# The first four tiles of each attention layer turned on TensorE, a written order for the first steps, and a flag check moved into the last filter's loop

## The chip, the cores and the metric

One Trainium2 chip, one core. TensorE (PE) multiplies matrices and can transpose 128x128 blocks; VectorE (DVE), ScalarE (ACT) and GpSimd (POOL) do the rest; SyncE (SP) issues nearly all DMAs. The metric is the device time of one execution in microseconds (us). The kernel before took 3790.33 us, the median of three runs (3786.84 to 3791.4).

## The reference

Two times attention and then a spectral filter, each on a layernormed input and added to it. Weights are the same in both layers.

```
x: (1, 2048, 1024)    32 heads of 32    float32
x = x + attn(layernorm(x));  x = x + filt(layernorm(x))     # twice
attn(x): q, k, v = x @ wqkv;  softmax(q k^T / sqrt(32)) v;  @ wo
filt(x): irfft2(rfft2(x) * (w_r + i w_i))
layernorm(x) = (x - mean) / sqrt(var + 1e-5)
```

## The kernel before

x lies in SBUF as 16 tiles of 128 rows by 1024 columns (`ap.x`, in the trace R). Float32 products are made of float16 halves: a number is split into a high part (`hi`, on ACT) and what is left (`lo`, on DVE), and a product is hi·hi + hi·lo + lo·hi (`split`, L167 and L168).

**The attention's prologue.** Each tile goes through `ln`: BN_STATS on its two halves (L111, L112), an aggregation, the root of the variance by a power on POOL (L120) and one Newton step on DVE (L121 to L124), a bias `lb`; then ACT writes the normed tile `xn` (L334), the split makes `hl` (hi and lo in float16), and two DMA transposes (L339) put them, turned, into `big`, the arrays `xh` and `xl` of four chunks of 512 rows. Out of these PE makes sums of 48 products for two tiles of v (`v_tiles`, L401; v0 to v7), and of 24 products for one chunk of k or q (`qk_chunk`, L357; k0 to k3, q0 to q3). Their order on PE is v0 v1 k0 q0 v2 k1 q1 v3 k2 q2 v4 k3 q3, the sums of the norms (L374), v5 v6, the first scores S (L586), v7. The norms go by POOL to a bias (L387) that the first exponential (L590) needs. In layer 0 the x tiles and the weights come by DMA meanwhile, in layer 1 x is in place and is written to memory beside the transposes (L341).

The sums use two PSUM banks by turns, `x` (v0, k0, v2, q1, ...) and `o` (v1, q0, k1, v3, ...). A sum starts only when the one before it in its bank is read out: v2 waits until k0's high part (ACT) and its low part (DVE, L168, written R<-x) have been taken. K's, Q's and V's first arrays lie in x's own tiles 0 to 7, so k0 may be taken out only when ACT has read tiles 6 and 7 for their xn.

The order on each engine is fixed when the kernel is built. In the prologue a scheduler chooses it by its own estimates of when things are ready; each engine then goes through its row in order and waits where something isn't ready. From the attention's main loop on (S, exp, PV at L596, sums at L609) the order is written out.

**The spectral filter** ends each layer. Its second part is a loop over 32 units (36 steps with the run-in and run-out), each with a weight load on SP (`loadw`), products on PE and three engines that follow; then come 16 steps of transposes and products (L982, L994), whose last adds to x are the rows L1005 to L1013. In layer 0 these adds are followed by layer 1's statistics.

**The flags.** Beside the work the kernel gathers whether a value left the range for which the split is good. `combine_flags` joins them after the last filter: two small PE instructions (L1161, L1166), DVE rows between and behind them, a conversion to an integer `fi` (L1170), and on every engine a load of it into a register (L1171) and a branch (L1223) round a general version that is not run here.

```
both banks:   bank(): odd calls psX ("x"), even calls psO ("o")
SP, layer 0:  x0 x1 wv(4 loads) wk(2) x2.. x5 ...   one x load per tile in ln
```

## Time and profile before

| what | value |
|---|---|
| median of three runs | 3790.33 us (3786.84 to 3791.4) |
| the profiled execution | 3789.62 us, of which the span is 3787.7 |
| PE busy | 3694.6 us (98%) |
| DVE busy | 3179.3 us (84%) |
| ACT busy | 2893.2 us (76%) |
| layer 0: first matmul, first S | 18.62, 111.37 us |
| layer 1: last adds of filter 0, first matmul, first S | 1893.81, 1908.19, 1994.18 us |
| last matmul of the last filter, end of span | 3774.83, 3787.7 us |

A row of the timeline reads: start, duration (both us), engine, line, operation, out<-in with the shapes, how many instructions the row groups, and in square brackets how long the engine had been idle ahead of it and what ended that. A row of the windows gives a stretch's bounds and length, the busy time (and instructions) of PE, of PE's weight loads, of DVE, ACT and POOL, the clock granted to PE as a part of full speed, the busy share of the DMA engines and GB/s.

### The profile page before, as it was taken

The page shows a single profiled execution, that of the slowest core. Times are in us where ns is not written, and L with a number is a line of the kernel's source. Part 1 is how long each engine was busy: PE and PEld are TensorE (multiplying, and loading weights), DVE is VectorE, ACT ScalarE, POOL GpSimd, SP SyncE. Part 2 cuts the span into 40 slices and gives each one's busy share as a digit, 9 for nine tenths or more (in the row PEclk, how much of TensorE's full clock was granted, in tenths as well). Part 3 has the DMA queues.
Part 4 walks back from the last instruction along what each step waited for, and adds up shares of the span by engine and source line. Part 5 has one row for each costly group of instructions (what it writes and reads, how often), then busy time and mean ns, then how long its engine had stood idle before and what let it go on. Part 6 is the DMA issues. An engine that isn't in the chain of part 4 may idle for free.

```text
span 3787.7 us, 79598 instructions
## 1 busy us (share of the span) xinstructions
PE 3694.6 (98%) x32951; PEld 1640.7 (43%) x32951; DVE 3179.3 (84%) x3824; ACT 2893.2 (76%) x3567; POOL 308.2 (8%) x386
## 2 busy tenths in 40 slices
PE   7999999999999999999989999999999999999998
PEld 4433433343344233378953334333433432333798
DVE  6799899989999988955658998999899999789554
ACT  5688888888888866658747888888888888666696
POOL 1000000000000000014410000000000000000143
PEclk9999999999999999999999999999999999999999
DMA  8000000000000211233270010001000002111433
GB/s 209 15 18 18 13 12 18 24 10 18 12 24 11 94 48 65 79 124 119 69 184 15 29 34 24 29 26 35 14 29 29 33 14 93 54 70 67 156 98 106
DMA packets 166868, 202.58 MB, mean 53 GB/s; under 512 B 75104, under 2 KB 120928, under 8 KB 165472
## 3 DMA queue, kind: packets, MB, share of 16 engines
q1 hardware_dynamic: 166208, 197.34, 16.3%
q8 instruction: 260, 4.26, 0.5%
q14 instruction: 112, 0.92, 0.1%
q10 hardware_dynamic: 288, 0.07, 0.0%
HBM read 132.35 MB, written 48.23 MB: 48 GB/s over the span
## 4 chain that ended last, share of the span: by engine, by line
PE 85%; DVE 6%; issue 4%; ACT 2%; DMA 1%; POOL 1%; SPq 0%; DVEq 0%; POOLq 0%; ACTq 0%
PE o L596 23%; PE s L586 19%; PE x L357 15%; PE x L401 7%; PE x L459 6%; PE ps L879 3%; PE s L459 2%; DVE R L609 2%; PE ps L823 2%; PE s L616 2%; PE ps L948 1%; PE ps L911 1%; PE ps L814 1%; PE ps L994 1%; PE ps L982 1%
## 5 line engine op out<-in xcount | busy, mean ns | idle before, releaser
L590 ACT ACTIVATE p<-s,bias 128x1024 f32<-128x1024 f32 x2048 | 2168.7, 1112 | 569.1 <-PE s L586 553.2
L609 DVE TENSOR_TENSOR R<-R,p 128x1024 f32<-128x1024 f32 x1792 | 2087.2, 1218 | 130.9 <-ACT p L590 127.6
L596 PE MATMUL o<-p,R 128*32 128x512 f32 x8192 | 985.0, 598 | 0.0
L357 PE MATMUL x<-big,wqk 128*128 128x512 f16 x2880 | 676.4, 380 | 1.7 <-ACT R L405 0.9
L586 PEld LDWEIGHTS <-R 32*128 32x128 f16 x12288 | 230.7, 92 | 752.9 <-issue 636.8
L357 PEld LDWEIGHTS <-wqk 128*128 128x128 f16 x3072 | 275.7, 98 | 419.6 <-issue 131.3
L596 PEld LDWEIGHTS o<-p,R 128*32 128x32 f32 x8192 | 213.7, 109 | 523.3 <-issue 523.3
L586 PE MATMUL s<-R 32*128 32x512 f16 x6144 | 430.2, 378 | 5.2 <-ACT p L590 3.3
L586 PE MATMUL s<-Q,R 32*128 32x512 f16 x6144 | 427.3, 377 | 4.6 <-DVE R L500 2.6
L401 PE MATMUL x<-wv,big 128*128 128x256 f16 x2784 | 331.8, 276 | 33.3 <-DMA big<-hl 33.3
L401 PEld LDWEIGHTS <-big 128*128 128x128 f16 x3072 | 292.8, 99 | 135.1 <-issue 58.6
L459 PE MATMUL x<-big 128*128 128x512 f16 x1050 | 241.6, 380 | 0.0
L382 POOL PARTITION_ALL_REDUCE mall<-mqk x16 | 45.2, 2826 | 2281.5 <-DVE mqk L376 2269.9
L459 PEld LDWEIGHTS <-big 128*128 128x128 f16 x1344 | 124.3, 98 | 176.4 <-issue 38.6
L607 DVE SCALAR_TENSOR_TENSOR R<-p 128x1024 f32<-128x1024 f32 x128 | 150.7, 1218 | 34.6 <-ACT p L590 34.6
L927 DVE TENSOR_TENSOR H<-G,H 128x512 f16<-128x512 f32 (+1 forms) x68 | 47.1, 692 | 116.6 <-ACT H L926 116.4
L872 ACT COPY U<-ps 64x256 f32<-64x256 f32 (+1 forms) x272 | 97.0, 357 | 9.4 <-PE ps L879 4.1
L879 PE MATMUL ps<-cbi,H 128*128 128x256 f16 (+1 forms) x792 | 98.8, 273 | 4.0 <-ACT H L926 2.7
L872 ACT COPY B<-ps 64x256 f32<-64x256 f32 (+1 forms) x272 | 97.0, 357 | 6.7 <-PE ps L879 3.2
L617 DVE STREAM_TRANSPOSE zt<-s 128x512 f32<-128x512 f32 x64 | 45.7, 714 | 62.8 <-PE s L616 62.7
L879 PE MATMUL ps<-cb,big 128*128 128x256 f16 x780 | 96.2, 273 | 0.0
L828 DVE TENSOR_TENSOR big<-ps,big 128x512 f16<-128x512 f32 x64 | 44.5, 695 | 57.8 <-ACT big L827 57.8
(431 smaller groups left out, 2952.0 us busy)
## 6 DMA issues: line engine op xcount, KB each, us to landing
wst<-in_wp SPq DMA_DIRECT2D x96, 256.0 KB, 3.1
R<-y SPq DMA_DIRECT2D x32, 512.0 KB, 5.2
w<-in_w SPq DMA_DIRECT2D x60, 256.0 KB, 2.6
od<-ohl SPq DMA_DIRECT2D x56, 256.0 KB, 2.4
big<-od SPq DMA_DIRECT2D x16, 896.0 KB, 6.4
y<-R SPq DMA_DIRECT2D x20, 512.0 KB, 2.6
R<-in_x SPq DMA_DIRECT2D x16, 512.0 KB, 5.8
wst<-in_wo SPq DMA_DIRECT2D x32, 256.0 KB, 2.9
```

Source lines behind the costliest of these rows:

```text
L357: nc.tensor.matmul(ps, a, b, start=d == 0 and i == 0, stop=d == 7 and i == 2)
L401: nc.tensor.matmul(ps[:, j], l, r, start=d == 0 and i == 0, stop=d == 7 and i == 2)
L459: nc.tensor.matmul(p, a, b, start=start and d == ds[0] and i == 0, stop=stop and d == ds[-1] and i == 2)
L586: nc.tensor.matmul(s[h // 2][:, h % 2], K[g][r, a, kt * 128:kt * 128 + 128], Q[g][r, b, c * 512:c * 512 + 512], start=i == 0, stop=i == 2)
L590: nc.scalar.activation(p, s[hf], AF.Exp, bias=bias[g], scale=SCALE / (SQ * SQ))
L596: nc.tensor.matmul(O[g, c][32 * h:32 * h + 32], V[g][:, kt, 32 * h:32 * h + 32], P[g, c, kt, h // 2][:, h % 2], start=kt == 0, stop=kt == ...
L607: nc.vector.scalar_tensor_tensor(acc[hf], P[g, c, 0, hf], 1e-34, p, op0=ALU.add, op1=ALU.add)
L609: last_add = nc.vector.tensor_add(acc[hf], acc[hf], p)
L616: nc.tensor.matmul(z[32 * h:32 * h + 32], cst["ones"], acc[h // 2][:, h % 2], start=True, stop=True)
L823: nc.tensor.matmul(pa[:, j], tt[:, j], mm[:, g], start=True, stop=True)
L872: nc.scalar.copy(ov[64 * r:64 * r + 64, a0:a0 + m, x], tl[64 * x:64 * x + 64, :m, r])
L879: nc.tensor.matmul(out, l, r, start=k == 0, stop=k == len(mm_) - 1)
```

## The change

Four things are changed.

1. Tiles 0 to 3 of both layers are turned on PE: eight float32 transposes of `xn` into PSUM (`turn_x`), out of which ACT takes the high and DVE the low part straight into `xh` and `xl` (`split_x`). `hl` and the DMA transposes stay for tiles 4 to 15.
2. These first steps have an order written out on PE, DVE and ACT. On DVE the Newton step of tile t+1 stands behind the low part of tile t (for tile 1 ahead of tile 0's), on PE the turn of tile t+1 stands between the matmuls of v0 or v1. In layer 1 tile 0's statistics and root stand among the last adds of filter 0. The rest of the prologue has a written order on PE alone; its other work is let go when the fourth tile's split has been issued (`issue_after`).
3. The sums run xh·w_hi (8 products), xh·w_lo (8), xl·w_hi (8) and no longer alternate. norm(k) stands ahead of 24 matmuls of v5, norm(q) behind them. SP's x loads stand early and in a row (x0, the four of wv, x1 to x3, wk, x4, wq, x5 to x15); in layer 1 the writes of x stand ahead of the transposes instead of beside them. The five looks for flags on the weights follow the prologue's last low part.
4. `combine_flags` is called in step 20 of the last filter's loop; at the end only the register load stays.

```diff
-    v, r, q = (sm.tile([128, n], F32, name=f"{c}{n}") for c in "vrn")
+def ln_pow(nc, sm, cst, mv, eng, n=1):
...
+def ln_newton(nc, sm, v, r, eng, n=1):
...
+def tile_root(nc, ap, cst, flags, layer, t):
+
+    mv = tile_stats(nc, ap, flags, layer, t)
+    v, r = ln_pow(nc, ap.sm, cst, mv, nc.vector)
+    yield
+    ln_newton(nc, ap.sm, v, r, nc.vector)
+    flags["rb"] = r, ln_bias(nc, ap.sm, mv, r)
+    yield
...
+    def save_x(ts):
+        for t in ts if layer else ():
+            nc.sync.dma_start(xin[t * 128:(t + 1) * 128, :], ap.x[:, t])
...
+    def turn_x(xn):
+        p = psS.tile([128, 2, 512], F32, name="s").rearrange("p h (d n) -> p (h d) n", n=128)
+        for d in range(8):
+            nc.tensor.transpose(p[:, d], xn[:, 128 * d:128 * d + 128], cst["ident"])
+        return p
+
+    def split_x(t, p, n):
+        c, o = t // 4, (t % 4) * 128
+        for d in range(0, 8, n):
+            r = split(nc, xh[c][:, d:d + n, o:o + 128], xl[c][:, d:d + n, o:o + 128], p[:, d:d + n], SX)
+        return r
...
-            if layer:
-                nc.sync.dma_start(xin[t * 128:(t + 1) * 128, :], ap.x[:, t])
...
+        for i, (a, b) in enumerate([(w[:, n, d], x[c][:, d]) for x, n in ((xh, 0), (xh, 1), (xl, 0)) for d in range(8)]):
+            nc.tensor.matmul(ps, a, b, start=i == 0, stop=i == 23)
...
+    with tc.manual_schedule(engines={mybir.EngineType.PE, mybir.EngineType.DVE, mybir.EngineType.Activation}):
...
+        xn = norm_x(0, *flags.pop("rb"))
+        for t in range(4):
+            p = turn_x(xn)
+            if t < 3:
+                m = tile_root(nc, ap, cst, flags, layer, t + 1)
+                next(m)
+                run(pre[0])
+                if t == 0:
+                    next(m)
+            ends = split_x(t, p, 4 if t == 0 else 8)
+            if t % 2:
+                if t < 3:
+                    next(m)
+                    xn = norm_x(t + 1, *flags.pop("rb"))
+                run(vk.pop(0))
+            else:
+                if t:
+                    next(m)
+                xn = norm_x(t + 1, *flags.pop("rb"))
+                steps(vk[0], 8)
+    with tc.manual_schedule(engines={mybir.EngineType.PE}):
+        with tc.issue_after(ends[0].ins), tc.issue_after(ends[1].ins):
+            run(pre[1])
+            ln(4, 2)
+            run(pre[2])
+            ln(6, 2)
+            for c in range(NCH):
+                for i, ph in enumerate(PH0[1:]):
+                    if c < 2:
+                        low = ln(8 + 4 * c + 2 * i, 2)
+                    run(qk_chunk(ph, c))
+                if c < 3:
+                    run(vk.pop(0))
+        save_x(range(8, 16))
+        norms()
+        steps(vk[0], 12)
+        norms()
...
+        if i == 20 and join:
+            join(ps)
...
+            m = iter(()) if i < 15 or flags is None else tile_root(nc, ap, cst, flags, 1, 0)
...
+                    if n == (1 if t.start else 3):
+                        next(m, None)
...
-        bad = combine_flags(nc, tc, cp, flags, cst)
+        bad = nc.values_load(flags["bad"][0:1, 0:1], min_val=0, max_val=1)
```

How rows move, first on ACT in layer 1, from the end of filter 0 on (`xn` the normed tile, `hl` its halves, `s` a PSUM tile with the turned xn, `big` the arrays xh and xl, `R<-x` and `R<-o` v0 and v1 taken out of their banks). Before:

```order
L334 ACTIVATE xn_21445<-R_91,lb1_21443,r1_21435 128x1024
L167 ACTIVATE hl_21447<-xn_21445 128x1024
L334 ACTIVATE xn_21466<-R_91,lb1_21464,r1_21456 128x1024
L167 ACTIVATE hl_21468<-xn_21466 128x1024
L334 ACTIVATE xn_21489<-R_91,lb2_21487,r2_21479 128x1024
L167 ACTIVATE hl_21491<-xn_21489 128x1024
```

And after:

```order
L360 ACTIVATE xn_21499<-R_92,lb1_21472,r1_21462 128x1024
L204 ACTIVATE big_88<-s_21501 128x4x128 x2
L360 ACTIVATE xn_21527<-R_92,lb1_21521,r1_21513 128x1024
L204 ACTIVATE big_88<-s_21546 128x8x128
L360 ACTIVATE xn_21570<-R_92,lb1_21568,r1_21558 128x1024
L452 ACTIVATE R_92<-x_21529 128x256 x2
L204 ACTIVATE big_88<-s_21606 128x8x128
L360 ACTIVATE xn_21630<-R_92,lb1_21628,r1_21618 128x1024
L204 ACTIVATE big_88<-s_21649 128x8x128
L452 ACTIVATE R_92<-o_21632 128x256 x2
```

ACT alternates xn and high part in both; but the high part now reads what PE has turned, so PE stands between the two rows of each tile.

On DVE in layer 1 the low part of k0 (`R<-x` with 512 columns) stands before among these rows (`st` the statistics of a tile, `r2`, `n2`, `v2` the Newton step of a pair of tiles, `fmv` means and variances):

```order
L168 SCALAR_TENSOR_TENSOR hl_21702<-xn_21700,hl_21702 128x1024
L122 TENSOR_TENSOR n2_21862<-n2_21862,v2_21860 128x2
L326 BN_AGGR fmv_76<-st_21915 128x2
L111 BN_STATS st_21919<-R_91 128x6
L123 TENSOR_SCALAR n2_21862<-n2_21862 128x2
L112 BN_STATS st_21919<-R_91 128x6
L168 SCALAR_TENSOR_TENSOR hl_21758<-xn_21756,hl_21758 128x1024
L168 SCALAR_TENSOR_TENSOR R_91<-x_21709,R_91 128x512
L124 TENSOR_TENSOR r2_21861<-r2_21861,n2_21862 128x2
```

And after:

```order
L205 SCALAR_TENSOR_TENSOR hl_21721<-xn_21719,hl_21721 128x1024
L127 TENSOR_TENSOR n2_21771<-r2_21768 128x2
L112 BN_STATS st_21825<-R_92 128x6
L128 TENSOR_TENSOR n2_21771<-n2_21771,v2_21767 128x2
L111 BN_STATS st_21934<-R_92 128x6
L205 SCALAR_TENSOR_TENSOR hl_21747<-xn_21745,hl_21747 128x1024
L129 TENSOR_SCALAR n2_21771<-n2_21771 128x2
L151 BN_AGGR fmv_76<-st_21825 128x2
L112 BN_STATS st_21934<-R_92 128x6
L130 TENSOR_TENSOR r2_21768<-r2_21768,n2_21771 128x2
L205 SCALAR_TENSOR_TENSOR R_92<-x_21793,R_92 128x512
L205 SCALAR_TENSOR_TENSOR hl_21754<-xn_21752,hl_21754 128x1024
```

Between the low part of tile 3 and that of k0 stand, after, 16 statistics of half tiles, the low parts of tiles 4, 5 and 6 and 25 small rows of roots and biases. In layer 0 it is 18 statistics, the same three low parts, four low parts of the weights of k and q, and one of q0.

On SP the last filter's end (`w` the weight loads of the loop, `mi` a constant of the last part, `fi` the joined flag) reads before:

```order
L855 DMA w_41855<-in_w 128x512
L855 DMA w_41916<-in_w 128x512
L855 DMA w_41978<-in_w 128x512
L977 DMA mi_42195<-in_mm_ 128x256
L1029 DMA out_0<-R_91 128x16x128 x7
L1027 DMA out_0<-R_91 128x8x128 x2
L1171 TENSOR_LOAD fi_42730
L1171 ISA x2
L1223 COMPARE_AND_BRANCH
```

And after:

```order
L936 DMA w_41450<-in_w 128x512
L1305 TENSOR_LOAD fi_82
L1305 ISA x2
L936 DMA w_41538<-in_w 128x512
L936 DMA w_41600<-in_w 128x512
```

SP's load of the flag has moved ahead of ten weight loads of the loop; the branch itself still stands behind the output's writes.

More of the change, by code (lines that the diff above doesn't have):

```diff
@@ L125, in ln_scale, with ln_bias, tile_stats @@
     return r
+def ln_scale(nc, sm, cst, mv, eng, n=1):
+    return ln_newton(nc, sm, *ln_pow(nc, sm, cst, mv, eng, n), eng, n)
+def ln_bias(nc, sm, mv, r, n=1):
+    b = sm.tile([128, n], F32, name=f"lb{n}")
+    nc.vector.scalar_tensor_tensor(b, mv[:, 0::2], -1.0, r, op0=ALU.mult, op1=ALU.mult)
+    return b
+def tile_stats(nc, ap, flags, layer, t):
+    if layer and t < NST:
+        st = flags["st"][:, t]
+        nc.vector.bn_stats(st[:, 1], ap.x[:, t, 512:1024])
+    else:
+        st = bn_stats(nc, ap.sm, ap.x[:, t])
+    mv = flags["mv"][:, layer * 16 + t]
+    nc.vector.bn_aggr(mv, st)
+    return mv
+def tile_root(nc, ap, cst, flags, layer, t):
[5 more added lines that the diff above has]
+    yield
 def ln_stats(nc, sm, cst, st, mv):
@@ L568, in attention, with steps @@
-    run(prep(phases[0]))
-    last_v = vk.pop()
-    if layer == 0:
-        for _ in range(5):
-            wts.look()
-    for v in vk:
-        run(v)
+    def steps(g, n):
+        for _ in range(n):
+            next(g, None)
+    with tc.manual_schedule(engines={mybir.EngineType.PE, mybir.EngineType.DVE, mybir.EngineType.Activation}):
+        steps(pre[0], 1)
+        for t in range(1, 4):
+            load_x(t)
+        steps(pre[1], 1)
+        load_x(4)
+        steps(pre[2], 1)
+        for t in range(5, 10):
+            load_x(t)
+        save_x(range(8))
+        if layer == 0:
+            m = tile_root(nc, ap, cst, flags, 0, 0)
+            for _ in range(2):
+                next(m)
+                steps(pre[0], 1)
+            steps(pre[0], 1)
+        xn = norm_x(0, *flags.pop("rb"))
[13 more added lines that the diff above has]
+                run(vk.pop(0))
+            else:
+                if t:
+                    next(m)
+                xn = norm_x(t + 1, *flags.pop("rb"))
+                steps(vk[0], 8)
@@ new lines, in attention @@
+    with tc.manual_schedule(engines={mybir.EngineType.PE}):
[15 more added lines that the diff above has]
+        norms()
+        run(prep(phases[0]))
+        if layer == 0:
+            with tc.issue_after(low.ins):
+                for _ in range(5):
+                    wts.look()
+        last_v = vk.pop()
+        for v in vk:
+            run(v)
@@ L1217, in build @@
             if layer:
-                spectral(nc, tc, ap, y, x, a, cst, True)
+                spectral(nc, tc, ap, y, x, a, cst, True, join=lambda ps: combine_flags(nc, ps, cp, flags, cst))
             else:
```

103 lines of the change are left out of this document (35 added, 68 removed).

## The prediction

> **What bounds the kernel now.** I read the page's head first, then the timeline of the two prologues and of the end, windows of 2 us for the clock, and for the end the waits by line and the DMA view.
>
> ```profile
> span 3787.7 us, 79598 instructions
> PE 3694.6 (98%) x32951; PEld 1640.7 (43%) x32951; DVE 3179.3 (84%) x3824; ACT 2893.2 (76%) x3567; POOL 308.2 (8%) x386
> ```
>
> PE is busy 98% of the span, so only the few places where it isn't can give time, and whatever makes it idle costs its full length. The change touches the two prologues, one step of the last loop and the end. For the prologues I measure from the last work ahead of them to the first S, since the main loop behind it is the same.
>
> ```profile
> 1893.81 5.12 DVE L1013 TENSOR_TENSOR R<-R,ps 128x512 f32<-128x512 f32 x12
> 1903.05 1.24 ACT L334 ACTIVATE xn<-R,lb,r 128x1024 f32<-128x1024 f32 x1 [10.55 <-DVE n L123]
> 1908.19 0.61 PE L401 MATMUL x<-wv,big 128*128 128x256 f16 x2 [12.80 <-DMA big<-hl]
> 1924.03 5.34 PE L357 MATMUL x<-big,wqk 128*128 128x512 f16 x24
> 1934.39 5.40 PE L401 MATMUL x<-wv,big 128*128 128x256 f16 x48
> 1945.60 5.34 PE L357 MATMUL x<-big,wqk 128*128 128x512 f16 x24 [0.63 <-ACT R L405]
> 1994.18 0.83 PE L586 MATMUL s<-R 32*128 32x512 f16 x12
> ```
>
> In layer 1 PE waits 12.80 us for the first transposes, then v2 starts at 1934.39 without a wait and nearly nothing is lost up to S. Layer 0:
>
> ```profile
> 8.06 1.87 ACT L167 ACTIVATE wv<-wst 128x512 f16<-128x512 f32 x3 [5.13 <-DMA wst<-in_wp]
> 11.26 1.24 ACT L334 ACTIVATE xn<-R,lb,r 128x1024 f32<-128x1024 f32 x1 [1.33 <-DMA wst<-in_wp]
> 18.62 0.61 PE L401 MATMUL x<-wv,big 128*128 128x256 f16 x2 [18.62 <-DMA big<-hl]
> 48.50 5.40 PE L401 MATMUL x<-wv,big 128*128 128x256 f16 x48
> 56.65 5.34 PE L357 MATMUL o<-big,wqk 128*128 128x512 f16 x24 [2.75 <-DVE R L168]
> 67.97 5.40 PE L401 MATMUL o<-wv,big 128*128 128x256 f16 x48 [0.80 <-DVE R L168]
> 111.37 0.83 PE L586 MATMUL s<-R 32*128 32x512 f16 x12
> ```
>
> Here k1 waited 2.75 us and v3 0.80 on low parts on DVE; from v3 on PE is dense. So the bank read-out by DVE already decides in layer 0.
>
> **The durations.** The serial work of a turned tile, from the timeline:
>
> ```profile
> 1923.49 1.21 DVE L168 SCALAR_TENSOR_TENSOR hl<-xn,hl 128x1024 f16<-128x1024 f32 x1
> 1924.69 0.68 DVE L112 BATCH_NORM_STATS2 st<-R 128x6 f32<-128x512 f32 x1
> 1925.29 1.21 DVE L168 SCALAR_TENSOR_TENSOR hl<-xn,hl 128x1024 f16<-128x1024 f32 x1
> 1926.42 0.16 DVE L123 TENSOR_SCALAR n<-n 128x2 f32<-128x2 f32 x1
> 47.49 0.67 DVE L168 SCALAR_TENSOR_TENSOR R<-x,R 128x512 f16<-128x512 f32 x1
> 1904.32 1.06 ACT L167 ACTIVATE hl<-xn 128x1024 f16<-128x1024 f32 x1
> 1869.77 1.34 PE L982 MATMUL ps<-ident,big 128*128 128x128 f32 x8
> 62.26 0.16 DVE L121 TENSOR_TENSOR n<-r 128x2 f32<-128x2 f32 x1 [0.87 <-POOL r L120]
> 63.27 1.23 ACT L334 ACTIVATE xn<-R,lb,r 128x1024 f32<-128x1024 f32 x1
> ```
>
> Back to back, from start to start, a half tile's statistics take 0.60 us on DVE (1924.69 to 1925.29), a low part 1.13 (1925.29 to 1926.42), a small row some 0.08 (the one at 1926.42 starts with the low part's end and its like follow at that pace; an estimate). From the Newton step's first row to xn are 1.01 us (62.26 to 63.27). One turned tile is then xn 1.24, eight transposes 1.34, high part 1.06, low part 1.13 and, since the next tile's Newton step stands behind that low part, 1.01: 5.78, and with some 0.1 of handover 5.9 us. Before, xn came every 2.2 to 2.6 us.
>
> **Layer 1.** The last adds end at 1898.93 (1893.81 + 5.12). Tile 0's statistics and two small rows now stand among them (+0.8), then come the Newton chain (1.01) with tile 1's half statistics in it (0.60) and a handover: xn0 at about 1901.5, 1.5 earlier than before. Tile 1's Newton precedes tile 0's low part, so xn1 follows after xn, turn and high part, 3.85 us. xn2 and xn3 each come a whole tile later, 6.4 (16 matmuls of v0 stand on PE ahead of turn 1) and 5.9: xn3 at 1917.7, its high part done at 1921.5, its low part at 1922.7. Now DVE works off what the order shows between the low parts of tile 3 and k0: 16 statistics (9.6), 3 low parts (3.4), 25 small rows (2.0), then k0's own 0.67. That is 15.7: v2 may start at 1938.5, with handovers 1939, as against 1934.39. PE itself would be ready about 1934.6: behind the high part of tile 3 it has half of v1 (2.6), k0 and q0 (10.4, as from 1924.03 to 1934.39). So PE gets a wait of 4.4 us, which is the first cost.
>
> The clock is the second. After the pause in layer 1 it was low in the windows:
>
> ```profile
> 1898.00:1900.00 2.00, 0.00 (x0) 0.00 (x0) 2.00 (x5) 0.00 (x0) 0.00 (x0) 0.52 1.02 403
> 1912.00:1914.00 2.00, 2.00 (x11) 1.39 (x10) 1.41 (x6) 1.97 (x3) 0.58 (x1) 0.50 0.84 181
> 1914.00:1916.00 2.00, 2.00 (x16) 1.59 (x14) 2.00 (x6) 1.97 (x3) 0.00 (x0) 0.71 0.81 273
> 1916.00:1918.00 2.00, 2.00 (x21) 1.80 (x19) 2.00 (x7) 1.06 (x2) 0.60 (x1) 1.00 1.16 262
> 20.00:22.00 2.00, 2.00 (x11) 1.45 (x10) 1.78 (x7) 0.00 (x0) 0.70 (x1) 1.00 0.99 269
> 32.00:34.00 2.00, 2.00 (x10) 1.41 (x11) 2.00 (x7) 1.97 (x3) 0.00 (x0) 0.50 0.98 186
> 30.98 0.61 PE L401 MATMUL o<-wv,big 128*128 128x256 f16 x2 [4.00 <-DMA big<-hl]
> ```
>
> At 0.50 PE ran 11 matmuls in 2 us, at 1.00 it ran 21. In layer 1 the fall came in 1898 to 1900, the rise after some 6 us of matmuls. In layer 0 the first matmuls also ran at the half rate (11 in 20 to 22, though the clock column prints 1.00), and after a pause of 4.00 us it was low again, while after the 2.75 us ahead of k1 it wasn't. In the changed kernel the first turns and half sums fall into that low clock: turn 0 takes 1.3 us more, 16 matmuls 1.75 more, part of turn 1 again, about 3.2 together on the chain of tiles (bounds 0, if PE's short pieces do not wait on each other, and 3.6, if turns 0 and 1 and the 16 matmuls are all slow). The new wait of 4.4 us lies just beyond the 4.00 that fell; I take 2 for the slow restart (bounds 0 and 2.5, from 1910 to 1915 in layer 1). Given back: the 0.63 ahead of q1 and about 1 on the norms' sums. S in layer 1 is later by 4.4 + 3.2 + 2 - 1.6 = 8.0 (bounds +2.8, without both clock terms, and +9).
>
> [...]
>
> **Layer 0.** The weights of v no longer wait for x1: a weight load lands first about 6.7, and ACT's xn0 comes at about 9.0 instead of 11.26. First turn 10.3, first matmul 13 to 14 instead of 18.62, a gain at the start. The tiles then follow as above (3.85, 6.3, 6.0): low part of tile 3 at 30, with the low clock 33. DVE has 18 statistics (10.8), 4 low parts of weights (2.7) and q0's (0.67), 3 of tiles (3.4), small rows (2.3) ahead of k0's: 20. v2 starts at 51.0 or, with the low clock, 53.9, against 48.50. PE has worked off k0 and q0 by about 44, so it waits 7 to 9 us, and restarts slowly (+2). Given back are DVE's waits on x:
>
> ```profile
> 46.88 0.70 DVE L111 BATCH_NORM_STATS2 st<-R 128x6 f32<-128x512 f32 x1 [1.51 <-DMA R<-in_x]
> ```
>
> x is all asked for early, so that wait and PE's 2.75 and 0.80 go. v2, k1, q1 are 15.8 us (5.40 and twice 5.18, half of 1924.03 to 1934.39), the slow restart 1 to 2 of it or more, and v3 stands at 67.8 or 71.7 against 67.97. Behind it a wait of about 1 on the norms' sums goes. S: -1.2 or +3.5; with the slow start likelier I take +2.4.
>
> **The norms.** norm(q) follows norm(k) by 24 matmuls of v5, half of a sum of 5.40, so POOL's all-reduce starts up to 2.7 later and with it the bias for the first exponential. v6's matmuls and S stand between and cover most: I take +0.5 for both layers together (0 to 2).
>
> **The rest of SP and of the order of products.** The sums keep their number of products, and x is written to memory off PE's path; I cost them at nothing, under the cover of DVE's row above (a late transpose of tiles 4 to 7 would add to k1).
>
> **The flag join.** Two small matmuls and the wait between them stand in the loop now; at the end the first took 0.27 and the wait 0.44 (rows below): +0.5, at most +4 if SP's load holds the weights.
>
> **The end.**
>
> ```profile
> 3771.76 3.07 PE L994 MATMUL ps<-mi,tt 128*128 128x128 f32 x26
> 3777.33 1.12 SPq L1027 DMA_DIRECT2D out<-R  x2
> 3777.45 0.27 PE L1161 MATMUL ft<-ident,f 128*6 128x128 f32 x1 [2.63 <-DVE R L1013]
> 3778.16 0.18 PE L1166 MATMUL fn<-sign,fa 6*1 6x1 f32 x2 [0.44 <-DVE fa L1163]
> L1171 PEldq TENSOR_LOAD <-fi x1: 1262/1262/1262, 3778.7 to 3778.7; - x1
> L1223 PEldq COMPARE_BRANCH  x1: 5195/5195/5195, 3780.1 to 3780.1; - x1
> out<-R SPq DMA_DIRECT2D x2, 512.0 KB, 5.1
> ```
>
> PE's register load (1.26) and branch (5.20) now start at the last matmul's end, 3774.83, not at 3778.7: done at 3781.3. Then the last output transfers end it: issued at 3777.33 and 3777.9 and 5.1 long, 3783.0. Behind the branch's end (3780.1 + 5.2 = 3785.3) the span had 2.4 us left; behind 3783.0 that makes 3785.4, which is 2.3 earlier (bounds -4, by PE's rows alone, and 0, if the close waits for something else).
>
> **The sum.** +2.4 + 8.0 + 0.5 + 0.5 - 2.3 = +9.1. The profiled execution took 3789.62 (span 3787.7 and 1.9 round it), so 3798.7. That execution lies 0.7 below the median of 3790.33, so the median becomes about 3799.
>
> **Rivals.** A measurement of this kernel can tell about 0.2% (7.6 us) from no change, so "same" is 3782.7 to 3797.9.
> (1) *The clock does not fall or rises early.* For: the pieces on PE are short, and the column printed 1.00 in 20 to 22. Against: 0.50 for 15 us in layer 1. Then layer 0 is -1.2, layer 1 +2.8, the norms +0.5, the flags +0.5, the end -2.3: +0.3, about 3790 or 3791, the same.
> (2) *DVE isn't full, faster.* If DVE skips through (statistics overlapped, low parts not late) v2 waits for nothing in either layer: layer 0's S comes at about 100.5 (from 13 on, seven sums of v at 5.40, eight of k and q at 5.18, four turns at 1.34 are 84.6, and 3 for slow starts), -11; layer 1 is -1.4 (PE ready at 1934.6 instead of 1934.39, less the 1.6 given back); norms, flags and end -1.3. That is 3776. Against it: DVE's rows back to back in 1898 to 1918, 2.00 of 2 us in three of the four windows of layer 1 above. It decides at v2: earlier than 48.5 and 1934.4 or not.
> (3) *SP's load of the flag holds the weight loads.* +4 on top of the forecast, 3803. For: it waits on an engine's result in SP's one row, ahead of ten loads. Against: loads run a unit or more ahead.
>
> **The chances.** Forecast, with (3) in it, 0.55; (1) 0.28; (2) 0.17. Faster is (2), the same (1), slower the forecast. The range leaves out (2) in both layers, but takes in (2) in layer 0 alone (-11 + 8.0 + 0.5 + 0.5 - 2.3 = -4.3, 3786) with 2 to spare, 3784; above it reaches to (3) with half of what the other high bounds add (1.0 and 1.1 for the layers, 1.5, 2.3), 3807. The forecast's own range is 3793 to 3807.
>
> **What would show it.** Right: v2 waits on DVE R<-x for some 4 us in layer 1 and 7 to 9 in layer 0, behind a row of statistics; xn every 6 us for tiles 1 to 3; the clock at 0.50 in turns 0 to 1; a first matmul at 13 to 14; the end 7 to 11 us behind the last filter matmul. Wrong: v2 without a wait, xn closer than 5 us, or a loop whose weight loads stall in step 20.

## The result and the profile after

The changed kernel took 3797.07 us (median of 13 runs, 3792.75 to 3801.21), the kernel before in the same comparison 3792.17 (13 runs): a ratio of 1.0014, interval 1.0005 to 1.0023. So it is slower by about 4.9 us, clear of noise, but less than the 0.2% that the prediction set as the bound of "the same". A second comparison on another occasion gave 1.0012 (1.0003 to 1.0021). The page after, its head:

```profile
span 3795.0 us, 79696 instructions
PE 3707.5 (98%) x33015; PEld 1650.6 (43%) x33015; DVE 3186.0 (84%) x3838; ACT 2895.2 (76%) x3569; POOL 303.8 (8%) x388
```

The timeline of PE in the changed kernel, layer 0:

```profile
9.81 1.97 PE L366 MATMUL s<-ident,xn 128*128 128x128 f32 x8 [9.81 <-ACT xn L360]
...
39.48 5.34 PE L406 MATMUL o<-big,wqk 128*128 128x512 f16 x24
54.52 6.74 PE L448 MATMUL x<-wv,big 128*128 128x256 f16 x48 [9.69 <-DVE R L205]
...
114.10 0.83 PE L667 MATMUL s<-R 32*128 32x512 f16 x12
```

PE begins at 9.81 instead of 18.62. It loses that lead again, most of it at v2: it waits 9.69 us for a row of DVE written R<-x, which is k0's low part, and v2 then takes 6.74 instead of 5.40. S comes at 114.10, 2.7 later than before. Layer 1, PE, ACT and DVE of the changed kernel:

```profile
1891.74 3.74 PE L1077 MATMUL ps<-mi,tt 128*128 128x128 f32 x32
1900.46 1.24 ACT L360 ACTIVATE xn<-R,lb,r 128x1024 f32<-128x1024 f32 x1 [7.88 <-DVE lb L140]
1901.76 1.97 PE L366 MATMUL s<-ident,xn 128*128 128x128 f32 x8 [6.27 <-ACT xn L360]
1905.61 1.23 ACT L360 ACTIVATE xn<-R,lb,r 128x1024 f32<-128x1024 f32 x1
1913.47 1.24 ACT L360 ACTIVATE xn<-R,lb,r 128x1024 f32<-128x1024 f32 x1 [2.19 <-DVE lb L140]
1919.05 1.24 ACT L360 ACTIVATE xn<-R,lb,r 128x1024 f32<-128x1024 f32 x1 [2.13 <-DVE lb L140]
1922.53 1.23 DVE L205 SCALAR_TENSOR_TENSOR big<-s,big 128x1024 f16<-128x1024 f32 x1 [3.51 <-ACT big L204]
1939.20 0.68 DVE L205 SCALAR_TENSOR_TENSOR R<-x,R 128x512 f16<-128x512 f32 x1
1939.93 7.79 PE L448 MATMUL x<-wv,big 128*128 128x256 f16 x48 [4.23 <-DVE R L205]
2000.56 0.83 PE L667 MATMUL s<-R 32*128 32x512 f16 x12
```

The four xn stand at 1900.46, 1905.61, 1913.47 and 1919.05. From the start of tile 3's low part (1922.53) to the start of k0's (1939.20) are 16.7 us, of which DVE is busy for 16.37, and v2 waits 4.23 us for that. The clock, in windows of 2 us, the columns as before:

```profile
1902.00:1904.00 2.00, 1.73 (x8) 1.32 (x7) 0.00 (x0) 0.24 (x1) 0.00 (x0) 0.50 1.03 408
1936.00:1938.00 2.00, 0.00 (x0) 0.00 (x0) 2.00 (x4) 2.00 (x4) 0.00 (x0) 1.00 0.83 188
1938.00:1940.00 2.00, 0.07 (x1) 0.07 (x1) 2.00 (x7) 1.52 (x3) 1.44 (x2) 0.51 0.92 205
1942.00:1944.00 2.00, 2.00 (x12) 1.38 (x10) 1.78 (x6) 1.97 (x2) 0.65 (x1) 0.50 0.82 184
1944.00:1946.00 2.00, 2.00 (x16) 1.62 (x15) 2.00 (x6) 1.97 (x3) 0.00 (x0) 0.79 0.55 123
```

It is at 0.50 in the first turn and again during v2. The end of the changed kernel, on PE and SP, and PE's wait between the two small products of the join inside the loop:

```profile
3780.24 3.74 PE L1077 MATMUL ps<-mi,tt 128*128 128x128 f32 x32
3786.49 1.76 SPq L1114 DMA_DIRECT2D out<-R  x2
L1306 PEldq COMPARE_BRANCH  x1: 4169/4169/4169, 3782.4 to 3782.4; - x1
3678.29 0.18 PE L1251 MATMUL ps<-sign,fa 6*1 6x1 f32 x2 [0.42 <-DVE fa L1249]
```

From the start of the last 32 products to the end of the span are now 14.76 us (3795.0 - 3780.24), where it was 16.61 (3787.7 - 3771.09): 1.85 less. PE's branch ends at 3786.6, well ahead. The last two output transfers, issued from 3786.49 on, take 5.3 to 6.1 us, so the last lands at about 3792.7, and the span ends some 2.3 us behind it: the output decides.

Each profile can be cut at four rows that all kernels share: the first S of layer 0, the start of the last 32 products of filter 0 (1891.65 before), the first S of layer 1, and the start of the last 32 products of filter 1. The stretches in us, and the medians of the runs. The medians come from several occasions, on which the kernel before took 3792.2 to 3793.5; the ratio compares with the kernel before on the same occasion:

| kernel | A: start to S, layer 0 | B: to filter 0's last products | C: to S, layer 1 | D: to filter 1's last products | E: to the end | median, us | ratio to before (interval) |
|---|---|---|---|---|---|---|---|
| before | 111.37 | 1780.28 | 102.53 | 1776.91 | 16.61 | 3792.17 | |
| changed | 114.10 | 1777.64 | 108.82 | 1779.68 | 14.76 | 3797.07 | 1.0014 (1.0005 to 1.0023) |
| changed_again | 114.03 | 1778.24 | 108.15 | 1779.83 | 14.85 | 3797.45 | 1.0012 (1.0003 to 1.0021) |
| join_only | 110.71 | 1779.80 | 103.23 | 1778.50 | 14.46 | 3790.86 | 0.9994 (0.9985 to 1.0003) |
| hold_stats | 110.67 | 1777.73 | 106.51 | 1780.59 | 14.60 | 3794.34 | 1.0000 (0.9991 to 1.0009) |
| stats_in_gaps | 106.72 | 1779.31 | 105.57 | 1778.31 | 14.69 | 3788.12 | 0.9986 (0.9977 to 0.9995) |
| more_banks | 112.42 | 1779.46 | 104.82 | 1777.33 | 14.57 | 3793.10 | 0.9997 (0.9988 to 1.0006) |
| warm_pe | 113.47 | 1777.13 | 106.47 | 1778.17 | 14.56 | 3795.22 | 1.0006 (0.9997 to 1.0016) |
| dma_turns | 119.44 | 1779.69 | 108.18 | 1781.77 | 14.42 | 3804.59 | 1.0030 (1.0017 to 1.0042) |
| early_roots | 113.11 | 1782.01 | 103.94 | 1781.18 | 14.36 | 3792.52 | 0.9992 (0.9983 to 1.0001) |
| early_roots_2 | 111.97 | 1778.67 | 104.27 | 1778.90 | 14.79 | 3790.50 | 0.9993 (0.9984 to 1.0002) |
| roots_two_ahead | 108.44 | 1778.76 | 99.52 | 1779.38 | 14.40 | 3784.33 | 0.9976 (0.9966 to 0.9985) |
| gaps_2 | 105.56 | 1778.59 | 104.73 | 1779.86 | 14.66 | 3785.70 | 0.9984 (0.9975 to 0.9993) |
| both_layers | 105.16 | 1780.79 | 100.37 | 1779.07 | 14.71 | 3782.07 | 0.9970 (0.9957 to 0.9982) |

A and C are what the prologues do. B and D hold the same work in all kernels but for the join in D; they differ by up to 5 us from profile to profile. Between before and changed, 1.1 of the 2.6 us in B are waits of PE (18.6 against 17.5 us in all, in the waits between 110 and 1890); where the rest lies stays open.

### The profile page after: what moved, and what is told of

Read it like the earlier page. It is cut to its first block, busy times and chain, and to the rows that moved or that the text cites. A ratio compares the mean times of both kernels' runs of the same rounds, so it can differ in the third digit from the quotient of the medians.

```text
span 3795.0 us, 79696 instructions
## 1 busy us (share of the span) xinstructions
PE 3707.5 (98%) x33015; PEld 1650.6 (43%) x33015; DVE 3186.0 (84%) x3838; ACT 2895.2 (76%) x3569; POOL 303.8 (8%) x388
## 4 chain that ended last, share of the span: by engine, by line
## 5 line engine op out<-in xcount | busy, mean ns | idle before, releaser
L909 DVE TENSOR_TENSOR big<-ps,big 128x512 f16<-128x512 f32 x64 | 44.5, 695 | 57.4 <-ACT big L908 57.4
```

## The experiments

All start from the changed kernel unless said otherwise. The theory was that v2 waits for DVE's row of statistics in front of k0's low part, with a slow restart behind it.

**join_only**: the kernel before, with nothing but the join of the flags in the last filter's loop.

```diff
+        if i == 20 and join:
+            join(ps)
...
-        bad = combine_flags(nc, tc, cp, flags, cst)
+        bad = nc.values_load(flags["bad"][0:1, 0:1], min_val=0, max_val=1)
```

> The kernel before with the fourth part of the change alone: the flags are joined in step 20 of the last filter's loop, the prologues are as before. Theory of the prediction: +0.5 in the loop and -2.3 at the end, 1.8 us less than before; the last matmul's end to the span's end falls from 12.9 us to about 11.0, as the changed kernel shows. Rival: the load on SP ahead of ten weight loads holds them, +4 in the loop, and the sum is +2. The prologues and the first filter must stand as before; where filter 0's end lies against the first S also tells how much two executions of the same code differ there (the changed kernel had lost 2.7 us at the first S and only 0.1 at the end of filter 0).

Stretch E fell by 2.15 us, D rose by 1.6, of which the join makes 0.8: the products around it (rows ps<-cb) take 2.13 us from start to start, and 1.31 without it. The time is 2.3 us lower by the ratio, with an interval that holds 0 and the expected 1.8, and not the rival's +2. PE waits for no DMA behind the join, so SP's load of the flag holds no weight load for long. A and C moved by -0.7 and +0.7, though nothing in them was touched: that is what two executions differ by.

**hold_stats**: the statistics of tiles 8 to 15 behind k0's low part.

```diff
+        lows[ph, c] = split(nc, t[:, 0], t[:, 1], ps, SQ / (SX * SW))[1]
...
-                    if c < 2:
-                        low = ln(8 + 4 * c + 2 * i, 2)
                     run(qk_chunk(ph, c))
+                    if c < 2:
+                        with tc.issue_after(lows[PH0[1], 0].ins):
+                            low = ln(8 + 4 * c + 2 * i, 2)
```

> The changed kernel, but the statistics of tiles 8 to 15 stand on DVE behind the low part of k0. Theory one (DVE's row is what v2 waits for): 8 statistics and their small rows, 5 to 6 us, leave the row ahead of k0's low part and of the low parts of tiles 4 and 5; v2 starts at about 48.5 instead of 54.5 in layer 0 and without a wait, about 1936 instead of 1939.9 counted from the same first turn, in layer 1, where the slow restart (2.4 us) goes too. Together 10 us less than the changed kernel, if no later sum has to wait; k2 is the place where it could, since tiles 8 to 11 come later. Rival (the wait is made by ACT, the transposes or the clock and not by DVE's row): v2 stays within 1 us of where it is.

The PE rows of hold_stats, layer 0 and layer 1, and two rows of DVE in layer 1:

```profile
50.48 7.35 PE L448 MATMUL x<-wv,big 128*128 128x256 f16 x48 [5.83 <-DVE R L205]
...
1933.48 5.40 PE L448 MATMUL x<-wv,big 128*128 128x256 f16 x48 [2.22 <-DVE R L205]
1957.51 5.34 PE L406 MATMUL x<-big,wqk 128*128 128x512 f16 x24 [3.02 <-DVE R L205]
...
1931.13 1.23 DVE L205 SCALAR_TENSOR_TENSOR hl<-xn,hl 128x1024 f16<-128x1024 f32 x1 [1.00 <-ACT hl L204]
1932.74 0.69 DVE L205 SCALAR_TENSOR_TENSOR R<-x,R 128x512 f16<-128x512 f32 x1 [0.39 <-ACT R L204]
```

The wait fell from 9.69 to 5.83 and from 4.23 to 2.22: DVE's row is a cause, and the rival is out as the whole cause. But half the wait stayed, and k2 now waits 3.02 us for what was put behind. By the ratios to the kernel before (1.0014 and 1.0000) some 5 of the expected 10 us were gained, by the medians of the two occasions 3. What holds v2 in layer 1 now is ACT: DVE is idle ahead of the low parts of tiles 4 to 6 and of k0's, each time for ACT, which works through xn of tiles 4 to 7, the high parts of tiles 4 to 6 and k0's high part in one row of 8.4 us (1924.32 to 1932.71). In the changed kernel that row ends at 1938.09, only 1.1 us ahead of the start of k0's low part. So moving rows on DVE gains little unless tile 4's root, and with it ACT's row, comes earlier too, as it did here (xn of tile 4 is 25.9 us behind the first turn, for 27.9 in the changed kernel).

**stats_in_gaps**: in addition the statistics of tiles 4 to 7 in the pauses that DVE makes during the turns.

```diff
-            tile_stats(nc, ap, flags, layer, t)
+            if t > 7:
+                tile_stats(nc, ap, flags, layer, t)
...
+            for u in ((), (4,), (5,), (6, 7))[t]:
+                tile_stats(nc, ap, flags, layer, u)
             ends = split_x(t, p, 4 if t == 0 else 8)
```

> As hold_stats, and besides the statistics of tiles 4 to 7 stand in the pauses that DVE makes while a tile is turned (tile 4 with tile 1's turn, 5 with 2's, 6 and 7 with 3's). Theory one: 8 more statistics leave the row, v2 waits for nothing in either layer: first S 10 us earlier in layer 0 (about 103) and 6 to 7 earlier in layer 1 than in the changed kernel, 15 us or so in all, and 10 less than the kernel before. Rival: the pauses are too short, the low parts of tiles 1 to 3 come later by what is put in front of them, and the chain of four tiles grows by 1 to 2 us each; then the gain is less than that of hold_stats.

PE in stats_in_gaps:

```profile
45.78 5.40 PE L449 MATMUL x<-wv,big 128*128 128x256 f16 x48 [1.67 <-DVE R L205]
69.31 5.34 PE L407 MATMUL x<-big,wqk 128*128 128x512 f16 x24 [1.68 <-DVE R L205]
...
106.72 0.83 PE L671 MATMUL s<-R 32*128 32x512 f16 x12
...
1930.34 5.40 PE L449 MATMUL x<-wv,big 128*128 128x256 f16 x48
1954.19 5.34 PE L407 MATMUL x<-big,wqk 128*128 128x512 f16 x24 [2.32 <-DVE hl L205]
```

v2's wait is gone in layer 1 and 1.67 in layer 0, v2 runs in 5.40, the first S is 7.4 and 3.3 us earlier than in the changed kernel. The chain of the four tiles did not grow (18.6 us from the first turn to the fourth in layer 1 in both kernels), so the rival fell too. With the statistics done earlier, tile 4's root is ready earlier, and ACT's row with it: xn of tile 4 follows the first turn by 24.4 us in layer 1, for 25.9 in hold_stats. 9 us less than the changed kernel, 5 less than before (0.9986): this version beats both. What is missing of the 15 is mainly the 1.67 that v2 still waits in layer 0, and k2, which now waits 1.7 and 2.3 us.

**more_banks**: v2, k1, q1 and v3 summed in the PSUM tiles of the turns.

```diff
             both.append(True)
+            if both[0] and 6 <= len(both) < 10:
+                return psS.tile([128, 2, 512], F32, name="s")[:, 0]
```

> The changed kernel, but v2, k1, q1 and v3 are summed in the three PSUM tiles that the turns have used, so that v2 needs no bank that k0 fills; the orders of DVE and ACT are otherwise left to the same rules. Theory of the bank (v2 waits for k0's read-out and nothing else): v2 starts as soon as q0 is done, at 44.8 in layer 0 and 1935.6 in layer 1, 9.7 and 4.2 us earlier, and the slow restarts go: 15 us less. Theory of the row: v2 also reads tiles 4 and 5, whose low parts stand in the same row behind the statistics (44.55 to 47.5 in layer 0, 1932.4 to 1935.6 in layer 1) and then need a transpose of 3.5 us: v2 comes no earlier than 51 and 1939, a gain of 3 and 1 us, and the low clock stays.

PE in more_banks:

```profile
46.85 7.08 PE L450 MATMUL s<-wv,big 128*128 128x256 f16 x48 [2.04 <-DMA big<-hl]
57.73 12.21 PE L408 MATMUL s<-big,wqk 128*128 128x512 f16 x48 [3.79 <-DMA big<-hl]
...
1942.13 12.09 PE L408 MATMUL s<-big,wqk 128*128 128x512 f16 x48 [2.26 <-DMA big<-hl]
```

Neither expectation held as written. The low parts of tiles 4 and 5 came when they had come before (from 44.5 and 46.4 us on in layer 0), but v2 started at 46.85 in layer 0 and without a wait at 1934.46 in layer 1. Its sums take all products of the high part first (the third part of the change), and the high parts are turned earlier than the low ones; that this is the reason is read from the order and was not run by itself. k1 then waited 3.79 and 2.26 us for the transposes of tiles 6 and 7, whose xn and low parts stand in the same row. S came 1.7 and 4.0 us earlier than in the changed kernel where the theory of the bank asked for 15 together: the bank was one of two things that hung on the row.

**warm_pe**: idle products in the pause.

```diff
+                if c == 0:
+                    d = psS.tile([128, 2, 512], F32, name="s")
+                    for _ in range(17 if layer else 40):
+                        nc.tensor.matmul(d[:, 0], W[PH0[2]][:, 0, 0], xh[0][:, 0], start=True, stop=True)
```

> The changed kernel with idle products in the pause ahead of v2: behind q0 PE makes 40 matmuls of 128x512 in layer 0 (8.6 us of a pause of 9.7) and 17 in layer 1 (3.7 of 4.2) whose sums nothing reads. Theory of the clock: the pause stays, but v2 runs at the full rate, 5.4 us instead of 6.74 and 7.79, so the first S is 1.3 and 2.4 us earlier, 3.7 in all. Rival (v2 is slow because its transposed tiles come in late, not by the clock): v2 keeps its 6.7 and 7.8 us, and the time stays.

```profile
54.38 5.40 PE L448 MATMUL x<-wv,big 128*128 128x256 f16 x48 [1.06 <-DVE R L205]
...
1937.58 5.40 PE L448 MATMUL x<-wv,big 128*128 128x256 f16 x48 [0.56 <-DVE R L205]
```

v2 runs at the full rate in both layers (5.40 us, PE rows of warm_pe above): the slow restart is the clock's, which stood at 0.50 during v2 in the changed kernel. In layer 0 it starts at its old place; in layer 1 it starts 1.2 us earlier, counted from the last products of filter 0 (46.98 against 48.19 us), so that layer's S does not measure the restart alone. S gained 0.6 in layer 0, where q1 then waited 0.69, and 2.3 (or 1.7 against the second profile) in layer 1. The time fell by 1.9 us by the medians and 3 by the ratios, within what the two intervals leave open.

**dma_turns**: tiles 0 to 3 by `hl` and DMA transposes in the new written order.

```diff
-            p = turn_x(xn)
+            hl = pp.tile([128, 2, 1024], F16, name="hl", tag="p")
...
-            ends = split_x(t, p, 4 if t == 0 else 8)
+            ends = split(nc, hl[:, 0], hl[:, 1], xn, SX)
+            for j, q in enumerate((xh, xl)):
+                nc.sync.dma_start(q[0][:, :, t * 128:t * 128 + 128], hl[:, j], transpose=True)
```

> The changed kernel, but tiles 0 to 3 are turned by DMA as before, with the written order of xn, high part, low part and Newton step kept; PE turns nothing. Theory of the serial chain: without the turn (and the hand-over to and from PE) a tile takes 4.5 us instead of 5.6, the low part of tile 3 comes 4 to 5 us earlier, DVE's row starts earlier by as much, and v2's wait in layer 1 goes with its slow restart: S 6 us earlier in layer 1 and 4 in layer 0, although the first matmul comes 2 us later. Then turning on PE costs time in this order. Rival (turning pays): the transposes take 3.5 us and share the queues with x, the first sums and with them k0 and q0 come 3 us later than now, and S does not come earlier.

PE and ACT of dma_turns, layer 0:

```profile
23.89 8.29 PE L448 MATMUL x<-wv,big 128*128 128x256 f16 x48 [23.89 <-DMA big<-hl]
...
32.21 0.66 ACT L452 ACTIVATE R<-x 128x256 f32<-128x256 f32 x2 [11.86 <-PE x L448]
```

My theory that the turn costs time in this order fell: the time is 7 us above the changed kernel's, and S is 5.3 later in layer 0 (in layer 1 the same). The first matmul came at 23.89, and since the written order has ACT read out v0 ahead of tile 2's high part, ACT stood 11.86 us behind v0. So in this order turning on PE pays, and the written order is made for it. What turning alone is worth is not settled by this, because the order around it would have to be another.

**early_roots** and **early_roots_2**: Newton and xn of tile t+1 ahead of the split of tile t. In early_roots_2 the hold is on `lows[PH0[1], c]`, so that tiles 12 to 15 stand behind k1's low part.

```diff
+        p = turn_x(xn)
         for t in range(4):
-            p = turn_x(xn)
             if t < 3:
                 m = tile_root(nc, ap, cst, flags, layer, t + 1)
                 next(m)
                 run(pre[0])
+                next(m)
+                xn = norm_x(t + 1, *flags.pop("rb"))
+                q = turn_x(xn)
             ends = split_x(t, p, 4 if t == 0 else 8)
+            p = q
...
+                        with tc.issue_after(lows[PH0[1], 0].ins):
```

> The changed kernel with the turns on PE kept, but the Newton step and xn of tile t+1 stand ahead of the split of tile t on DVE and ACT for all tiles (the change does so for tile 1 alone), turn t+1 stands ahead of the matmuls that read tile t, and the statistics of tiles 8 to 15 stand behind k0's low part. Theory of the serial chain: then a tile costs what its busiest engine takes, DVE's 2.9 us (1.2 statistics, 1.1 low part, 0.6 small rows), the low part of tile 3 comes 8 us earlier in layer 1, PE is dense from tile 0's first matmuls on and v2 waits for nothing: from the first turn to S 88 us instead of 98.8 in layer 1; in layer 0, where x still arrives, S at about 101 instead of 114. 20 us less than the changed kernel. Rival (another row takes over): k2 waits for tiles 8 to 11, whose low parts stand behind 16 statistics, and gives back 3 to 5 us in each layer.

> As early_roots, but the statistics of tiles 12 to 15 stand behind k1's low part and so behind the low parts of tiles 8 and 9. If k2's wait in early_roots comes from the burst of 16 statistics, 8 of them (5 us) leave the row ahead of it and the wait goes, 3 to 5 us in each layer; if it comes from the transposes or from ACT, nothing changes.

PE, then DVE, of early_roots in layer 1:

```profile
1905.13 3.65 PE L366 MATMUL s<-ident,xn 128*128 128x128 f32 x16 [6.27 <-ACT xn L360]
1913.89 1.09 PE L366 MATMUL s<-ident,xn 128*128 128x128 f32 x8 [3.27 <-ACT xn L360]
1920.40 1.09 PE L366 MATMUL s<-ident,xn 128*128 128x128 f32 x8 [1.92 <-ACT xn L360]
...
1909.73 0.68 DVE L147 BATCH_NORM_STATS2 fst<-R 128x6 f32<-128x512 f32 x1
1911.57 0.16 DVE L127 TENSOR_TENSOR n<-r 128x1 f32<-128x1 f32 x1 [0.73 <-POOL r L120]
```

From turn 2 to turn 3 are 6.5 us, more than in the changed kernel, and S comes 93.9 us behind the first turn, not 88. The expectation was wrong in one point: tile 2's statistics and power still stood behind tile 0's low part on DVE (1909.73), and tile 3's behind tile 1's, so the chain through a low part into the next root was only put in another order. The second hold removed most of k2's wait (2.13 to 0.79 in layer 1, 1.05 to none in layer 0), as its expectation had it.

**roots_two_ahead**: the roots of tiles 1 and 2 ahead of tile 0's low part, tile 3's ahead of tile 1's.

```diff
+        rb = [root(1)]
+        p = turn_x(xn)
         for t in range(4):
+            if t < 2:
+                rb.append(root(t + 2))
+            if t < 3:
+                xn = norm_x(t + 1, *rb.pop(0))
+                q = turn_x(xn)
             ends = split_x(t, p, 4 if t == 0 else 8)
+            p = q
```

> early_roots missed because the statistics and the power of tile t+2 still stood behind the low part of tile t+1 (a tile took 6.5 us from turn to turn). Here the whole root (statistics, power, Newton) of tiles 1 and 2 stands ahead of tile 0's low part and that of tile 3 ahead of tile 1's, xn of tile t+1 ahead of tile t's high part, and the holds are those of early_roots_2. If the chain through one tile's low part into the next tile's root is what spaces the turns, the spacing falls to some 3.5 us (DVE: 1.2 statistics, 1.2 small rows, 1.1 low part), tile 3's high part comes 5 us earlier than in stats_in_gaps in layer 1, and S follows the first turn by about 90 us there instead of 95.2 and 98.8 (in the changed kernel); layer 0, where x comes by DMA, gains 3 to 6 on the changed kernel's 114. 15 to 20 us less than the changed kernel in all. Rival: the spacing stays at 5.5 and more, because ACT or the hand-over between the engines makes it, and the gain is that of early_roots_2.

PE of roots_two_ahead:

```profile
48.75 6.84 PE L448 MATMUL x<-wv,big 128*128 128x256 f16 x48 [3.00 <-DVE R L205]
...
1897.20 3.67 PE L366 MATMUL s<-ident,xn 128*128 128x128 f32 x16 [6.27 <-ACT xn L360]
1909.41 1.09 PE L366 MATMUL s<-ident,xn 128*128 128x128 f32 x8 [1.92 <-ACT xn L360]
1926.99 5.40 PE L448 MATMUL x<-wv,big 128*128 128x256 f16 x48 [0.89 <-DVE R L205]
1986.72 0.83 PE L670 MATMUL s<-R 32*128 32x512 f16 x12
```

Four turns in 13.3 us (1897.20 to 1910.5) instead of 19.7, and S 89.5 us behind the first turn: the serial chain through the low part was the cost of the turned tiles. 13 us less than the changed kernel where 15 to 20 were expected, 0.9976 of the kernel before.

**gaps_2**: stats_in_gaps with the second hold (the edit of early_roots_2).

> stats_in_gaps with the statistics of tiles 12 to 15 behind k1's low part. If k2's wait there (1.68 and 2.32 us) comes from the burst of 16 statistics ahead of the low parts of tiles 8 and 9, it goes as it went from 1.05 to none and 2.13 to 0.79 between early_roots and early_roots_2: 3 us less than stats_in_gaps, 3785.

A fell to 105.56 and C to 104.73; k2 waits for nothing in layer 0 and 0.79 us in layer 1. 3785.70, as expected to a microsecond.

**changed_again**: the changed kernel once more.

> The changed kernel once more, beside the two above on one chip. Its first profile lost 2.7 us by the first S of layer 0, and had them back at the end of filter 0 although no instruction there differs; other kernels regained 0.5 to 2.6 us in that stretch. If that is scatter of single executions, v2's waits of 9.7 and 4.2 us and the two S stand within 0.5 us of the first profile, while the stretch from S to the end of filter 0 and the main loop of layer 1 differ by 1 to 3. If it is an effect of the change, they repeat.

The waits of v2 came out at 9.68 and 4.23, A and C within 0.7. But B again came out 2 us shorter than before, and D again 2.9 longer. So the change may have a part in these two stretches; with a single profile of the kernel before, it isn't shown. In D, one wait differs in both profiles of the changed kernel: between 3155 and 3225 us S waits 1.8 us for the reduced norms (`mqk`) where it waited 0.5 before. But all of PE's waits in that stretch make 2.7 us before and 3.1 after, so this explains 0.4 of D's 2.8 us and the join 0.8; the rest stays open, and so does where B's 2 us come from.

**both_layers**: layer 0 as gaps_2, layer 1 as roots_two_ahead.

> Layer 0 as in gaps_2 (statistics of tiles 4 to 7 in the pauses), layer 1 as in roots_two_ahead. If the two prologues' gains stand on their own, S comes at 105.6 in layer 0 and 89.5 us behind the first turn in layer 1, and the time is 3 us below roots_two_ahead: about 3781, 0.9968 of the kernel before. Rival (layer 0's gain is lost again in the main loop or the first filter): as roots_two_ahead, 3784.

A 105.16, C 100.37, 3782.07 us: 0.9970 of the kernel before, 15 us less than the changed kernel, and the lowest of all medians. Its interval overlaps that of roots_two_ahead, so the time alone doesn't settle the rival; that A fell from 108.44 to 105.16 does speak for the gain in layer 0.

The third part of the change (the order of the products, of the x loads and of the writes of x) was not run alone, so its share in A and C is not known.

## Why the prediction was right or wrong

Forecast were 3799 us and slower; measured 3797.07 and slower by 4.9 us. The absolute time was met to 2 us, but of the difference of 9.1 that was forecast only a little over half came. That the time was met so closely is partly luck: the kernel before was put too low, at a median of 3790.33 over three runs where 13 gave 3792.17, and the difference was put too high, and the two errors have opposite signs. The two profiled spans differ by 7.3 us, and 2.5 of that is how far the profiled execution of before lay below its kernel's median. By its time alone the result stands midway between the forecast (+9.1) and rival (1) (+0.3); the traces decide between them, and they show the forecast's mechanism.

- **v2's wait, layer 1** was forecast at 4.4 us up to 1939, and was 4.23 up to 1939.93. The row of DVE from the end of tile 3's low part to the end of k0's was counted right (15.7 us forecast, 16.1 measured), and hold_stats and stats_in_gaps show that it is the cause. What ended the row was not only k0's low part itself: the roots of tiles 6 and 7 stand in it too, without which ACT may not read k0 out, and ACT's own row behind them ends only 1.1 us earlier (hold_stats), which the prediction did not count; more_banks shows that beside the bank the transposes of tiles 4 to 7 hang on that row.
- **v2's wait, layer 0** was forecast at 7 to 9 us and was 9.69; S was forecast 2.4 later, and came 2.7 later. The prediction has a slip here: with the slow start its own terms give +2.7 (71.7 - 67.97 - 1), where it writes +3.5. v3 came at 71.45, and S with +2.7 as these terms say.
- **The chain of tiles**: forecast spacings of xn of 3.85, 6.4 and 5.9 us and 3.2 more by the low clock; measured 5.15, 7.86 and 5.58. That is 2.4 more than without the clock's term; that all of it is the clock is argued from the rows at 0.50 and was not tested alone. xn0 came 1.0 earlier than forecast.
- **The slow restart** of 2 us was 2.4 and, in the second profile, 1.7 (v2 in 7.07) in layer 1, and 1.3 in layer 0; warm_pe shows it to be the clock, which stood at 0.50 in the changed kernel. Rival (1), that the clock does not fall, is out. The prediction took 4.4 us as just beyond the wait of 4.00 us behind which the clock was low in the kernel before. V2 was slow behind both waits of 4.23 us (7.79 and 7.07 for 5.40), but in more_banks sums were slow behind waits of 2.04 and 2.26 us too, shorter than the 2.75 us that left the clock at 1.00 in the kernel before.
- **Layer 1's sum** of 8.0 was too high: C rose by 6.3 and 5.6. The mis-sized terms are the clock in the chain (2.4 for 3.2) and the start of xn0 (1.0 earlier), 1.8 us in all.
- **The norms**: +0.5 forecast. The first exponentials, before and then after, ACT in both layers:

```profile
115.86 2.12 ACT L590 ACTIVATE p<-s,bias 128x1024 f32<-128x1024 f32 x2 [3.72 <-POOL bias L387]
1998.16 2.12 ACT L590 ACTIVATE p<-s,bias 128x1024 f32<-128x1024 f32 x2 [3.22 <-POOL bias L387]
```

```profile
118.81 2.12 ACT L671 ACTIVATE p<-s,bias 128x1024 f32<-128x1024 f32 x2 [3.95 <-POOL bias L436]
2005.83 2.12 ACT L671 ACTIVATE p<-s,bias 128x1024 f32<-128x1024 f32 x2 [4.51 <-POOL bias L436]
```

  They followed S by 4.49 and 3.98 us, and now by 4.71 and 5.27: +0.2 and +1.3, together 1.5, within the forecast's bounds of 0 and 2 but three times its value.
- **The flag join**: +0.5 forecast, +0.8 found (2.13 us for 1.31 around the join, in the changed kernel as in join_only), of which 0.42 is PE's wait for DVE's row between the two small products. The end: -2.3 forecast, -1.85 found, and by the named mechanism (the output decides).
- **What was not in the sum**: B and D, 2.6 less and 2.8 more in the changed kernel's profile (D with the join and the waits named under changed_again), nearly cancel. That they do is luck.
- **Rivals.** (2), v2 without a wait, did not occur; stats_in_gaps shows that it would have been faster, as the rival says, but 0.9986 (5 us) is a little over a third of its price of 14; the next waits, k2's 1.7 and 2.3 us, are a part of what is missing. (3) did not occur.

## What to carry to other kernels

Where an engine turns, splits and evacuates for another, the row of the helping engine is the thing to count: from the last piece of the new chain to the first read-out that a PSUM bank waits for, every instruction in between has a price, and moving the ones that are not yet needed behind that read-out, or into the engine's pauses, was worth over twice what the change itself cost (gaps_2, 11 us for 4.9). Then the next engine's row is the one to count, here ACT's. A chain over tiles costs its longest loop through all engines; to shorten it, whole roots had to stand two tiles ahead here, one tile ahead only reordered it. And a sum built on one execution carries that execution's luck: cut several profiles at the same rows before differences of 2 us are believed.

## What the runs showed of the hardware

The length of a wait alone did not decide whether PE ran slow behind it. Behind waits of 1.67 (stats_in_gaps), 2.22 (hold_stats), 2.75 (the kernel before) and 3.02 us (hold_stats) the sums took 5.40 and 5.34 us; behind waits of 3.00, 3.69, 4.16 and 4.23 us the sums of v2 took 6.84, 7.07, 6.84 and 7.79 (in roots_two_ahead, dma_turns, early_roots and the changed kernel). But in more_banks sums were slow behind waits of 2.04 and 2.26 us too: v2 took 7.08, and k1 with q1 12.09 instead of 10.5. Where the granted clock was read, it goes with that: 1.00 behind the 2.22 and the 2.75 us, 0.50 behind the 4.23 us, and 0.58 and 0.57 behind the 3.00 us (48 to 50 and 50 to 52, v2 from 48.75 on).

The windows of 0.5 us in which the clock of the changed kernel fell or rose, and the one in which that of the kernel before fell in layer 1:

```profile
47.00:47.50 0.50, 0.00 (x0) 0.00 (x0) 0.50 (x1) 0.00 (x0) 0.50 (x1) 0.54 1.17 270
57.00:57.50 0.50, 0.50 (x6) 0.39 (x4) 0.50 (x3) 0.47 (x2) 0.00 (x0) 0.72 1.27 290
...
1900.00:1900.50 0.50, 0.00 (x0) 0.00 (x0) 0.33 (x3) 0.04 (x1) 0.33 (x1) 0.98 1.03 410
1910.50:1911.00 0.50, 0.50 (x5) 0.42 (x4) 0.00 (x0) 0.50 (x1) 0.00 (x0) 0.78 1.08 410
1938.00:1938.50 0.50, 0.00 (x0) 0.00 (x0) 0.50 (x4) 0.50 (x2) 0.28 (x1) 0.53 1.25 282
1944.50:1945.00 0.50, 0.50 (x5) 0.36 (x4) 0.50 (x2) 0.50 (x1) 0.00 (x0) 0.65 0.00 0
```

```profile
1898.00:1898.50 0.50, 0.00 (x0) 0.00 (x0) 0.50 (x3) 0.00 (x0) 0.00 (x0) 0.58 0.99 393
```

Between 1.00 and 0.50, the mean of a window puts the falls of the changed kernel at 47.0, 1900.5 and 1938.0 and its rises at 57.3, 1910.7 and 1944.9. The falls came 2.2, 5.0 and 2.3 us into PE's waits of 9.69, 6.27 and 4.23 us, and 2.7 us into the wait of 12.80 us in the kernel before. The rises came 2.8, 9.0 and 4.9 us behind the first matmul after the wait. So neither came at a fixed time from PE's stop or start; what else places them is not shown by these runs, nor why 2.04 us were enough in one run and 3.02 us not in another.

What v2 lost behind a fall varied from 1.3 to 2.6 us with the same instructions (6.74 and 7.79 in the two layers of the changed kernel, 7.98 in layer 0 of early_roots_2). It is half of the time that v2 spent at the low clock: 2.8 us in layer 0 of the changed kernel for 1.3 lost, 4.9 in layer 1 for 2.4, and 3.0 in layer 0 of roots_two_ahead for 1.4.
